# A third written order of all steps ahead of the experts, with the dilated unit 0 second

## The chip, the cores and the metric

The program runs on one core of a Trainium2 chip. The metric is the device time of one execution, in microseconds (us). The kernel before took 530.35 us, the median of three runs (530.16 to 531.51). One execution was profiled; its span is 528.5 us.

## What is computed

Attention over q, k, v of batch 2, 8 heads, 576 positions and depth 64: heads 0 to 3 see a plain causal window of 32, heads 4 to 7 a window of 128 in which every fourth position counts. Its 1152 x 512 result goes through a layer `h = x @ w_in` (512 x 1024), `solu = h * softmax(h)`, a layer norm over the 1024, scaled by g_ln, and `@ w_out` (1024 x 512). Four experts follow:

```
p = domain_probs / (domain_probs.sum(-1, keepdims=True) + 1e-09)
for e in range(4):
    h = np.maximum(x @ w1[e], 0.0)          # 512 x 1024
    out += p[:, e:e + 1] * (h @ w2[e])      # 1024 x 512
```

Every large product is done as three products of a high and a low part, so each weight and each activation is split in two before TensorE (PE) uses it.

## The kernel before

All that stands ahead of the experts is cut into steps, and one string, ORDER, lists them; a loop reads the string and lets each named generator run to its next `yield`. The order of the string is therefore the order in which instructions enter every engine's queue, and each engine works its own queue strictly in that order. SyncE (SP) issues every DMA. A "+" behind a step flips a switch for that one step: with it, some operations go to VectorE (DVE) in place of ScalarE (ACT), or to GpSimd (POOL) in place of DVE. The steps:

- `lP`, `lD`, `lvp`, `lvd` load q/k and v of one attention unit (L147, L150, L155). A unit is a third of the sequence of four heads of one batch: `UP.t.b` plain, `UD.t.b` dilated, 12 in all. In DMA names `qkD01` is batch 0, third 1.
- `UP`, `UD`: scores on PE (mask L262, q times k L271), maximum, subtraction, exponential, sum, reciprocal, division (L279, L281, L284, L286, L288, L290), the transpose of the weights on PE (L309, tile `pt`) or through memory, weights times v on PE (L320), and the split of the result into `xhi` (L170, L172) and `xlo` (L246). In this text QK, Tr and PV name the three PE parts.
- `lI.j`, `VI.j`: block j of w_in is loaded (L205, L208; 128 rows; block 0 in two halves, `lI.0` and `lI.4`) and converted from 64 bits: two ACT passes (L186, L188), two DVE operations (L190, L192), an addition (L194), then the split into `wh` (L172) and `wl` (L221). `lO`, `VO` do the same for w_out (`wh4` to `wh7`).
- `H.t`, t from 0 to 8: token tile t (128 rows) times w_in on PE (L350), four quarters, one for each block j; then maximum (L355), exponential (L357), product (L359), scaling (L362 on ACT or L364 on DVE).
- `T.t`: transpose of tile t. Tiles 3 to 8 go through memory: DVE shuffle into the one buffer `st4` (L395, L397), DMA out (L402, L405), ACT square (L407), DMA back into one of two `et` buffers (L411, L414), split into `hh` (L170, L172) and `hl` (L419).
- `X.c.d`: three token tiles times half of w_out on PE (L432), 48 matmuls in four parts of twelve, then the copy into `xf` (L170, L172).
- `F.n`: n matmuls on a constant tile (L84), whose result is not used.
- `WP`, `XQ`, `WV`, `u`, `d`: expert weights, split of xf, and the expert products on PE (L545, L617).

PSUM has two score/transpose buffers (`pa`) and two for H and X (`pm`); v of the plain units has two buffers (`vp`). A step that needs one waits for the reader of the one used two allocations before.

Of the kernel before, what the change touches and what calls it, by code (L numbers as in the profile page):

```python
# [27 lines left out]
ORDER = """
lP.0.0+ F.10 UP.0.0 UP.0.0+ lI.0 UP.0.0 lD.0.0 VI.0 VI.0 VI.0+ VI.0 F.4 UD.0.0 UP.0.0 UP.0.0+ lI.4 VI.0 VI.4+ UD.0.0 UP.0.0+ VI.4 UD.0.0+ UD.0.0+ lD.1.0+ VI.4
VI.4 VI.4+ lP.1.0+ F.3 UD.1.0 UD.1.0 UD.1.0+ UD.0.0 UD.0.0 UD.1.0+ UP.1.0 UP.1.0 UD.1.0 UD.1.0+ UP.0.0 VI.0 UP.1.0+ lD.2.0+ F.1 UD.2.0+ UD.2.0 lP.2.0 F.1  # L30
UP.2.0 UD.0.0+ UD.2.0 VI.4 UP.1.0+ UP.1.0+ lI.1+ UP.1.0+ VI.1+ VI.1+ UD.1.0+ lvd.1.0+ UP.2.0 UP.2.0+ UP.2.0 UD.1.0 VI.1+ VI.1 F.3 UP.0.0 UP.1.0 UD.1.0 VI.4+
F.1 UD.1.0+ UD.1.0+ UP.0.0 lI.2+ UD.1.0+ VI.0+ lvp.0.0+ UP.0.0 VI.2+ VI.2 UP.0.0 UP.0.0+ VI.1+ F.3 H.0+ VI.2 VI.2+ UD.2.0 VI.1 VI.1 UD.0.0 UD.0.0 UP.2.0+
UP.1.0 lI.3 UP.1.0 lvd.0.0 UD.0.0+ lvp.1.0 UP.1.0 lvp.2.0+ H.0+ UD.2.0+ VI.3 UD.0.0 UD.0.0 UP.1.0 UP.1.0 VI.3+ UD.2.0 VI.3 lP.0.1 UP.0.1 H.1 H.1 VI.2+ VI.2
UP.0.1 UP.0.1+ UP.0.1+ lO.0.0+ VO.0.0 VI.3 UD.2.0+ UD.2.0 UD.2.0 VI.3 VI.3 VI.3+ VI.2 lD.0.1+ UD.0.1 UD.0.1 UD.0.1+ lvp.0.1 lD.1.1+ UP.0.1 UP.2.0+ lvd.2.0+
UD.1.1 VO.0.0 lO.0.1 VO.0.1 UP.0.1 H.0 UD.1.1 VO.0.0 UD.2.0 UD.2.0 VO.0.0 VO.0.0+ H.0 UP.2.0+ lO.1.0+ lD.2.1 UD.2.0 H.0+ UD.0.1 UD.0.1+ endE+ UD.1.1+ VO.0.1+
VO.0.1+ H.0+ H.0 H.1 H.1 misc+ UP.0.1+ UP.0.1 UD.0.1+ UD.0.1+ H.1+ UP.2.0 UD.1.1 UD.0.1+ UD.0.1 UP.0.1 UP.0.1 UP.2.0 H.0+ UP.0.1 UP.0.1+ VO.0.1+ UD.1.1
lvd.1.1 UP.2.0 VO.0.1+ H.2 UP.2.0 lvd.0.1+ UP.2.0 UD.1.1 H.1+ H.1+ UD.1.1+ VO.0.0+ VO.0.0+ VO.0.1+ VO.0.1+ UD.2.1 UD.2.1+ VO.1.0+ VO.1.0 VO.1.0+ VO.1.0 lP.2.1
VO.1.0+ T.0 H.1+ lvp.2.1+ UD.2.1 lO.1.1+ UD.0.1+ T.0+ T.0 UD.1.1+ H.2+ H.2+ UD.2.1+ UD.1.1 T.1+ T.1+ T.1 H.3+ UD.2.1+ T.0+ UD.2.1+ T.1+ VO.1.0 VO.1.0+ VO.1.1+
VO.1.1 UP.2.1+ UP.2.1+ VO.1.1+ UP.2.1+ H.2+ UD.0.1 H.2 UD.0.1 lvp.1.1+ VO.1.1+ H.3+ UD.0.1+ lO.2.0+ VO.2.0 VO.2.0 UP.2.1 UP.2.1 UD.1.1 lP.1.1+ UD.2.1+ UD.2.1+
VO.1.1+ H.2+ H.3+ UD.1.1 UD.1.1 VO.2.0+ VO.2.0+ VO.2.0+ H.3 UD.1.1 H.3+ UP.2.1+ lO.2.1+ T.2 T.2 VO.1.1+ VO.1.1 T.2 T.2 VO.2.1+ VO.2.1+ UD.2.1+ VO.2.1+ H.4+  # L40
UP.2.1+ UP.2.1 H.4 H.4 UP.1.1+ VO.2.1+ UP.1.1+ UD.2.1+ UP.1.1 H.4 UP.1.1+ UP.1.1 UP.1.1 UP.1.1 X.0.1+ lO.3.0 VO.3.0 lvd.2.1 UP.2.1 VO.2.1+ UP.1.1+ VO.2.0+
VO.2.0 VO.2.1+ VO.2.1+ X.0.0 VO.3.0+ VO.3.0 VO.3.0+ VO.3.0 lO.3.1 VO.3.1 VO.3.1 UD.2.1+ VO.3.1+ VO.3.1 UP.2.1 VO.3.1 VO.3.0 H.4+ VO.3.1 VO.3.0+ VO.3.1 X.0.1+
UP.2.1 UP.1.1+ UP.1.1+ UD.2.1 UD.2.1 UP.1.1+ endA T.4 X.0.1 T.4+ T.4 H.3+ T.3+ T.3+ UP.1.1+ UP.1.1 H.5+ T.4+ T.3+ T.3+ H.5+ H.5+ H.5+ H.5+ H.5 X.0.0+ X.0.0
UP.2.1+ UP.2.1+ T.5+ T.5+ T.3+ H.6+ H.6+ T.4 T.4+ T.5 H.6 H.6+ T.3+ H.8 H.6 T.6 T.5+ T.6 H.8 H.8 T.5+ H.8+ H.8 T.8+ T.8+ T.6 T.6 H.7+ H.7 H.7 H.7 H.7 T.7+
T.7+ T.7+ T.6+ T.6 T.8+ T.8+ T.5+ X.1.0 X.1.0+ sc X.1.0 T.8+ T.8 T.7 X.1.1 X.1.1+ X.1.1 T.7+ T.7 endH XQ.0+ XQ.0 XQ.0 XQ.0 XQ.0 XQ.0 XQ.0 XQ.0 lW.0 WP.0+
WP.0+ WP.0 WP.0 WP.0 WP.0+ X.2.0 XQ.0 XQ.0 XQ.0 XQ.0+ XQ.0 XQ.0 XQ.0 WP.0+ WP.0 WP.0+ WP.0 WP.0 WP.0 WP.0+ WP.0 WP.0 X.2.1+ WP.0+ lW.1 WP.0 XQ.0 WP.0 X.2.0+
XQ.1 X.2.1 XQ.1 XQ.1 XQ.1 XQ.1 XQ.1 lV.0+ u.0+ u.0 u.0+ u.0 u.0 u.0+ u.0 u.0 u.0 endX u.0 u.0+ u.1+ u.0 XQ.1 XQ.1 u.1 WP.1+ WV.0 u.0+ u.0 u.0 WP.1 WV.0 u.0
u.0 u.0+ u.0 u.1+ u.0+ u.0+ u.0 u.0+ u.1 WV.0 WV.0 lV.1 u.0+ u.1+ u.1 lW.2 XQ.1 u.1+ u.1 XQ.1 XQ.1 XQ.1 d.2 d.2 XQ.1+ XQ.1 XQ.1 XQ.1+ WP.1+ d.0 d.0+ u.1+ u.1
u.1+ WP.1+ u.1+ u.1+ u.1+ u.1 u.1+ d.1+ d.1 WP.1 WP.1 u.1 u.1 u.1 u.1+ WP.1 WP.1+ WP.1 WP.1 WP.1 WP.1 WP.1+ WP.1 d.3+ WP.1 WP.1+ WP.1 d.3 WP.1 u.1 u.1 u.1+
u.1  # L50
"""
# [735 lines left out]
```

## Time and profile before

| what | value |
|---|---|
| median of three runs | 530.35 us |
| span of the profiled execution | 528.5 us |
| PE busy | 515.0 us (97%) |
| DVE busy | 356.9 us (68%) |
| ACT busy | 191.7 us |
| POOL busy | 187.3 us |
| DMA moved | 46.44 MB |

The page gives no total for the profiled execution besides its span; the median of the runs is 1.85 us above that span. PE busy counts the `F` matmuls too. Shares of the whole span hide the stages: PE is short of work ahead of about 30 us and has short gaps between 86 and 133 us, and from about 140 us, where the experts follow, it has none in the 20-us window shown below.

### The profile page before, as it was taken

What the parts mean: (1) busy time and instruction counts of PE and PEld (TensorE: products, weight loads), DVE (VectorE), ACT (ScalarE), POOL (GpSimd) and SP (SyncE); (2) the same over time, 40 slices, a digit from 0 to 9 for tenths busy, and PEclk for the clock granted to TensorE, in tenths of its full rate; (3) what the DMA queues carried; (4) which work ended last, traced back from release to release, by engine and by line L of the source; (5) the groups of instructions that cost most, each with busy time, mean ns of one, the idle gap of its engine ahead of it and who ended that gap; (6) DMA issues with size and microseconds to landing.
All of it is one profiled execution on the core that took longest, in us unless ns stands there. A gap on an engine that the chain in (4) does not pass through costs nothing.

```text
span 528.5 us, 9419 instructions
## 1 busy us (share of the span) xinstructions
PE 515.0 (97%) x3971; PEld 459.0 (87%) x3971; DVE 356.9 (68%) x474; ACT 191.7 (36%) x295; POOL 187.3 (35%) x130
## 2 busy tenths in 40 slices
...
GB/s 311 364 239 211 242 175 97 112 141 211 16 159 141 19 2 35 126 1 1 159 1 1 0 160 0 1 141 20 2 0 161 1 0 81 0 1 1 1 81 99
DMA packets 24490, 46.44 MB, mean 88 GB/s; under 512 B 4480, under 2 KB 9088, under 8 KB 24064
## 3 DMA queue, kind: packets, MB, share of 16 engines
...
## 4 chain that ended last, share of the span: by engine, by line
PE 87%; DMA 7%; DVE 4%; ACT 1%; SPq 1%; issue 0%; DVEq 0%; ACTq 0%
PE pa L617 19%; PE pm L617 18%; PE pm L545 17%; PE pa L545 17%; PE pm L350 7%; PE pm L432 6%; DMA vp<-in_vp_dram 2%; PE pa L320 2%; DMA et<-dt 2%; DMA draw<-in_moe_w_in_dram 1%; DMA dt<-st 1%; PE pa L271 1%; DVE e L359 1%; DVE e L364 1%; PE pa L381 1%; DVE st L397 0%
## 5 line engine op out<-in xcount | busy, mean ns | idle before, releaser
L558 DVE SCALAR_TENSOR_TENSOR hl<-ct,hh 128x512 fp32r<-128x512 f32 (+1 forms) x64 | 63.6, 1012 | 35.3 <-ACT hh L556 35.3
L556 ACT ACTIVATE hh<-ct 128x512 fp32r<-128x512 f32 (+1 forms) x64 | 42.1, 682 | 48.7 <-DVE ct L588 20.7
L617 PE MATMUL pa<-wl,hh 128*128 128x512 f32 (+1 forms) x148 | 57.3, 387 | 0.0
L617 PE MATMUL pa<-wh,hh 128*128 128x512 f32 (+1 forms) x148 | 57.3, 387 | 0.0
L617 PE MATMUL pa<-wh,hl 128*128 128x512 f32 (+1 forms) x148 | 57.1, 386 | 0.0
L545 PE MATMUL pm<-xoh,hl 128*128 128x256 f32 (+1 forms) x192 | 56.8, 296 | 0.0
L545 PE MATMUL pa<-xoh,hl 128*128 128x256 f32 (+1 forms) x192 | 56.8, 296 | 0.0
L545 PE MATMUL pm<-xol,hh 128*128 128x256 f32 (+1 forms) x192 | 56.8, 296 | 0.0
L545 PE MATMUL pa<-xol,hh 128*128 128x256 f32 (+1 forms) x192 | 56.8, 296 | 0.0
L545 PE MATMUL pm<-xoh,hh 128*128 128x256 f32 (+1 forms) x192 | 56.8, 296 | 0.0
L545 PE MATMUL pa<-xoh,hh 128*128 128x256 f32 (+1 forms) x192 | 56.8, 296 | 0.0
L617 PE MATMUL pm<-wl,hh 128*128 128x512 f32 (+1 forms) x144 | 55.7, 387 | 0.0
L617 PE MATMUL pm<-wh,hh 128*128 128x512 f32 (+1 forms) x144 | 55.7, 387 | 0.0
L617 PE MATMUL pm<-wh,hl 128*128 128x512 f32 (+1 forms) x144 | 55.6, 386 | 0.0
L464 POOL TENSOR_TENSOR wl<-wl,wh 128x1024 fp32r<-128x1024 f32 x7 | 16.9, 2414 | 95.3 <-ACT wh L172 95.3
L622 DVE SCALAR_TENSOR_TENSOR xf<-pm,pr,xf 128x512 f32<-128x512 f32 (+1 forms) x32 | 23.6, 738 | 31.1 <-PE pm L617 31.1
L464 POOL TENSOR_TENSOR hl<-sw,hh 128x512 fp32r<-128x512 f32 x22 | 33.5, 1522 | 30.3 <-ACT hh L172 27.6
L622 DVE SCALAR_TENSOR_TENSOR xf<-pa,pr,xf 128x512 f32<-128x512 f32 (+1 forms) x32 | 23.6, 738 | 30.3 <-PE pa L617 30.3
L172 ACT CAST wh<-wl 128x1024 fp32r<-128x1024 f32 x16 | 16.8, 1052 | 71.0 <-PE pa L617 40.5
L572 POOL TENSOR_TENSOR ct<-ct,ct 128x512 f32<-128x512 f32 (+1 forms) x15 | 21.4, 1426 | 48.1 <-ACT ct L570 42.9
L545 PEld LDWEIGHTS pm<-xoh,hh 128*128 128x128 f32 x192 | 36.4, 190 | 0.3
L545 PEld LDWEIGHTS pm<-xol,hh 128*128 128x128 f32 x192 | 36.4, 190 | 0.3
...
## 6 DMA issues: line engine op xcount, KB each, us to landing
...
```

What stands on the lines that cost most here:

```text
L172: nc.scalar.copy(out, in_)
L271: nc.tensor.matmul(ps[32 * g:32 * g + 32, j, 64 * m:64 * m + 64], lhsT=qt[rows, h, xq:xq + 32], rhs=kt[rows, h, xq:xq + 64], start=False, ...
L320: nc.tensor.matmul(po[64 * (g % 2):64 * (g % 2) + 64, j, o:o + 32], lhsT=vt[rows, m, g, :], rhs=pt[rows, m, g, :], start=True, stop=True)
L350: nc.tensor.matmul(pm[:, n, :], lhsT=xx[:, kk, cols], rhs=ww["in", kk][:, 512 * n:512 * n + 512], start=(n_ == 0 and i < 2), stop=(n_ == K ...
L432: nc.tensor.matmul(pm[:, dd, 0:CW], lhsT=w_, rhs=x_[:, f, :], start=(f == 0 and i == 0), stop=(f == KF - 1 and i == 2))
L464: pick().tensor_tensor(out=out, in0=a, in1=b, op=op)
L545: nc.tensor.matmul(ps[:, ff, 0:n], lhsT=a[:, kk, fc], rhs=b[:, kk, :], start=kk == 0 and m == 0, stop=kk == 1 and m == 2)
L556: nc.scalar.activation(out=hv, in_=src, func=AF.Relu)
L558: nc.vector.scalar_tensor_tensor(out=lv, in0=src, scalar=0.0, in1=hv.bitcast(F32), op0=ALU.max, op1=ALU.subtract)
L572: poolv().tensor_tensor(out=c12, in0=c21, in1=c22, op=ALU.add)
L617: nc.tensor.matmul(po[:, 0, 0:dn], lhsT=h_[:, f, cols], rhs=w_, start=(f == 0 and i == 0), stop=(f == 3 and i == 2))
L622: nc.vector.scalar_tensor_tensor(out=acc[:, t, dc], in0=po[:, 0, 0:dn], scalar=pr[:, t, e:e + 1], in1=acc[:, t, dc], op0=ALU.mult, op1=ALU ...
```

## The change

Only the string ORDER differs; every step of it is done in both kernels, 542 in each. The new string is one line shorter, so a line of the code has a number one less in the kernel after (L350 is L349). Its first line before and after:

```diff
-lP.0.0+ F.10 UP.0.0 UP.0.0+ lI.0 UP.0.0 lD.0.0 VI.0 VI.0 VI.0+ VI.0 F.4 UD.0.0 UP.0.0 UP.0.0+ lI.4 VI.0 VI.4+ UD.0.0 UP.0.0+ VI.4 UD.0.0+ UD.0.0+ lD.1.0+ VI.4
+lP.0.0+ lD.0.0 UP.0.0 lI.4 lD.1.0+ UP.0.0+ UD.0.0 F.3 lI.0 UP.0.0 UP.0.0 F.3 UD.0.0 VI.4+ lP.1.0+ lI.1+ UD.1.0 VI.4 VI.0 UP.0.0+ UP.0.0+ UD.0.0+ VI.4 VI.4
...
```

The F matmuls are 26 in both (10, 4, 3, 1, 1, 3, 1, 3 before; 3, 3, 1, 1, 1, 10, 4, 3 after). By the switches, DVE has 460 instructions where it had 465, POOL 134 for 127, ACT 274 for 276, in the part that the string orders.

First place: SP's queue of DMAs at the start of the program, before the change (`draw1` is block 1 of w_in, 1 MB; `draw0` has block 0 in two halves of 0.5 MB; a q/k unit is 0.43 or 0.46 MB, a v unit 0.39 MB):

```order
L147 DMA qkP00_107<-in_qkp_dram 128x832
L208 DMA draw0_202<-in_moe_w_in_dram 128x512
L147 DMA qkD00_110<-in_qkd_dram 128x896
L205 DMA draw0_202<-in_moe_w_in_dram 128x512
L147 DMA qkD01_111<-in_qkd_dram 128x896
L147 DMA qkP01_108<-in_qkp_dram 128x832
L147 DMA qkD02_112<-in_qkd_dram 128x896
L147 DMA qkP02_109<-in_qkp_dram 128x832
L208 DMA draw1_394<-in_moe_w_in_dram 128x1024
L150 DMA vd01_114<-in_vd_dram 128x768
L208 DMA draw2_455<-in_moe_w_in_dram 128x1024
L155 DMA vp_460<-in_vp_dram 128x768
L208 DMA draw3_520<-in_moe_w_in_dram 128x1024
L150 DMA vd00_113<-in_vd_dram 128x768
L155 DMA vp_550<-in_vp_dram 128x768
```

Here `qkD00` is third and block 1 of w_in ninth. SP's queue at the same place after the change:

```order
L146 DMA qkP00_107<-in_qkp_dram 128x832
L146 DMA qkD00_110<-in_qkd_dram 128x896
L204 DMA draw0_191<-in_moe_w_in_dram 128x512
L146 DMA qkD01_111<-in_qkd_dram 128x896
L207 DMA draw0_191<-in_moe_w_in_dram 128x512
L146 DMA qkP01_108<-in_qkp_dram 128x832
L207 DMA draw1_238<-in_moe_w_in_dram 128x1024
L146 DMA qkD02_112<-in_qkd_dram 128x896
L154 DMA vp_332<-in_vp_dram 128x768
L207 DMA draw2_410<-in_moe_w_in_dram 128x1024
L146 DMA qkP02_109<-in_qkp_dram 128x832
L149 DMA vd01_114<-in_vd_dram 128x768
L149 DMA vd00_113<-in_vd_dram 128x768
L154 DMA vp_458<-in_vp_dram 128x768
L154 DMA vp_482<-in_vp_dram 128x768
L146 DMA qkD10_119<-in_qkd_dram 128x896
L207 DMA draw3_558<-in_moe_w_in_dram 128x1024
```

Block 1 of w_in moves from ninth to seventh place, the dilated unit 0 from third to second, v of the plain unit 0 from twelfth to ninth, and q/k of the plain unit 2 (`qkP02`) from eighth to eleventh, behind three blocks of w_in; block 3 (`draw3`) moves from thirteenth to seventeenth.

Second place: PE around the first two quarters of H.0 (`wh0`, then `wh1`; `pa` rows are transposes, PVs and scores of attention units), before the change:

```order
L350 MATMUL pm_497<-wh0_206,xhi_90 128x512 x2
L350 MATMUL pm_497<-wl0_207,xhi_90 128x512 x2
L350 MATMUL pm_497<-wh0_206,xlo_91 128x512 x2
L309 MATMUL pa_509<-ident_74,pd1_126 128x128 x3
L309 MATMUL pa_516<-ident_74,pd0_125 128x128 x3
L320 MATMUL pa_525<-pt_513,vd00_113 64x32 x24
L320 MATMUL pa_552<-pt_522,vp_550 64x32 x24
L350 MATMUL pm_497<-wh1_397,xhi_90 128x512 x2
L350 MATMUL pm_497<-wl1_398,xhi_90 128x512 x2
L350 MATMUL pm_497<-wh1_397,xlo_91 128x512 x2
```

Between the two quarters stand two transposes and two PVs. PE around the same two quarters after the change:

```order
L270 MATMUL pa_431<-qkP02_109 32x64 x24
L308 MATMUL pa_465<-ident_74,pd2_127 128x128 x3
L349 MATMUL pm_473<-wh0_234,xhi_90 128x512 x2
L349 MATMUL pm_473<-wl0_235,xhi_90 128x512 x2
L349 MATMUL pm_473<-wh0_234,xlo_91 128x512 x2
L308 MATMUL pa_486<-ident_74,pd1_126 128x128 x3
L319 MATMUL pa_491<-pt_470,vd01_114 64x32 x24
L319 MATMUL pa_518<-pt_516,vd00_113 64x32 x24
L349 MATMUL pm_473<-wh1_335,xhi_90 128x512 x2
L349 MATMUL pm_473<-wl1_336,xhi_90 128x512 x2
L349 MATMUL pm_473<-wh1_335,xlo_91 128x512 x2
```

The second PV of a plain unit (`vp_550`) and one transpose no longer stand ahead of the second quarter; the scores of `qkP02`, which stood far ahead of the first quarter, now stand close before it.

Third place: PE where H.5 begins (`pm_1454`), before the change:

```order
L432 MATMUL pm_1232<-hh_942,wh7_1334 128x384
L432 MATMUL pm_1232<-hl_943,wh7_1334 128x384
L432 MATMUL pm_1232<-hh_942,wl7_1335 128x384
L320 MATMUL pa_1365<-pt_1330,vp_954 64x32 x24
L320 MATMUL pa_1397<-pt_1392,vp_1075 64x32 x24
L350 MATMUL pm_1454<-wh0_206,xhi_90 128x512 x2
L350 MATMUL pm_1454<-wl0_207,xhi_90 128x512 x2
L350 MATMUL pm_1454<-wh0_206,xlo_91 128x512 x2
L350 MATMUL pm_1454<-wh1_397,xhi_90 128x512 x2
```

X.0.1 (`pm_1232`) ends and two PVs follow before H.5. PE where H.5 begins (`pm_1301`) after the change:

```order
L431 MATMUL pm_1269<-hh_974,wh5_1081 128x384
L431 MATMUL pm_1269<-hl_975,wh5_1081 128x384
L431 MATMUL pm_1269<-hh_974,wl5_1082 128x384
L349 MATMUL pm_1301<-wh0_234,xhi_90 128x512 x2
L349 MATMUL pm_1301<-wl0_235,xhi_90 128x512 x2
L349 MATMUL pm_1301<-wh0_234,xlo_91 128x512 x2
L349 MATMUL pm_1301<-wh1_335,xhi_90 128x512 x2
L349 MATMUL pm_1301<-wl1_336,xhi_90 128x512 x2
L349 MATMUL pm_1301<-wh1_335,xlo_91 128x512 x2
```

H.5 stood behind both halves of X.0.1 and the last two PVs; it now stands between the two halves of X.0.1 (`pm_1269`), ahead of those PVs and of all of X.0.0. From H.6 on PE's order is the same in both: H.6, H.8, H.7, X.1.0, X.1.1, X.2.0, X.2.1, the expert products.

DVE's queue from the shuffle of tile 5 (`st4_1518`) to the maximum of H.7 (`pm_1607`), before the change:

```order
L395 STREAM_TRANSPOSE st4_1518<-e_1486 128x8x4x32
L170 CAST hh_1439<-et1_1471 128x8x128
L355 TENSOR_REDUCE nmx_83<-pm_1526 128x1
L359 SCALAR_TENSOR_TENSOR e_1551,nsum_85<-e_1551,pm_1526 128x1024
L364 TENSOR_SCALAR e_1551<-e_1551,nsum_85 128x1024
L397 STREAM_TRANSPOSE st4_1587<-e_1551 128x8x4x32
L355 TENSOR_REDUCE nmx_83<-pm_1559 128x1
L170 CAST hh_1439<-et1_1589 128x8x128
L359 SCALAR_TENSOR_TENSOR e_1593,nsum_85<-e_1593,pm_1559 128x1024
L364 TENSOR_SCALAR e_1593<-e_1593,nsum_85 128x1024
L397 STREAM_TRANSPOSE st4_1599<-e_1593 128x8x4x32
L355 TENSOR_REDUCE nmx_83<-pm_1607 128x1
```

Among the rows of tiles 6 and 8 stand two casts into `hh_1439`. DVE's queue from the shuffle of tile 5 (`st4_1487`) to the maximum of H.7 (`pm_1603`) after the change:

```order
L394 STREAM_TRANSPOSE st4_1487<-e_1450 128x8x4x32
L354 TENSOR_REDUCE nmx_83<-pm_1517 128x1
L358 SCALAR_TENSOR_TENSOR e_1543,nsum_85<-e_1543,pm_1517 128x1024
L363 TENSOR_SCALAR e_1543<-e_1543,nsum_85 128x1024
L396 STREAM_TRANSPOSE st4_1585<-e_1543 128x8x4x32
L354 TENSOR_REDUCE nmx_83<-pm_1557 128x1
L358 SCALAR_TENSOR_TENSOR e_1591,nsum_85<-e_1591,pm_1557 128x1024
L363 TENSOR_SCALAR e_1591<-e_1591,nsum_85 128x1024
L396 STREAM_TRANSPOSE st4_1600<-e_1591 128x8x4x32
L354 TENSOR_REDUCE nmx_83<-pm_1603 128x1
```

The two casts into `hh_1439` (tiles 3 and 5) are no longer in DVE's queue between these tiles; they are ACT's. The lo part of tile 6 (`hl`), which was DVE's behind H.7's work, is POOL's.

## Rows read from the trace of the kernel before

**Rows 1.** Windows of the span: PE, PEld, DVE, ACT, POOL busy; granted clock, DMA share, GB/s
```profile
10.00:20.00 10.00, 7.38 (x210) 4.48 (x210) 8.47 (x21) 5.50 (x10) 5.55 (x5) 0.83 1.03 414
...
20.00:30.00 10.00, 8.35 (x210) 6.80 (x211) 8.31 (x14) 7.88 (x13) 5.77 (x2) 0.83 0.82 299
...
60.00:80.00 20.00, 19.96 (x236) 17.49 (x235) 19.40 (x35) 14.46 (x25) 5.10 (x4) 1.00 0.55 174
...
140.00:160.00 20.00, 20.00 (x141) 20.00 (x141) 16.60 (x23) 9.55 (x14) 6.80 (x6) 1.00 0.31 106
```

**Rows 2.** PE's timeline up to 45 us: start, us, engine, line, operation, tiles
```profile
29.91 0.63 PE L350 MATMUL pm<-wl,xhi 128*128 128x512 f32 x2
...
30.90 0.33 PE L262 MATMUL pa<-mask,identb 128*128 128x192 bf16 x2
...
31.81 0.73 PE L350 MATMUL pm<-wh,xhi 128*128 128x512 f32 x2
...
39.84 0.62 PE L350 MATMUL pm<-wl,xhi 128*128 128x512 f32 x2
...
42.12 0.61 PE L350 MATMUL pm<-wh,xhi 128*128 128x512 f32 x2
...
43.49 0.82 PE L309 MATMUL pa<-ident,pd 128*128 128x128 f32 x6
...
44.55 1.60 PE L320 MATMUL pa<-pt,vp 64*64 64x32 f32 x96 [0.24 <-ACT pt L172]
```

**Rows 3.** ACT's timeline, the converting passes of w_in's blocks 1, 2 and 3
```profile
17.70 1.13 ACT L186 ACTIVATE draw<-draw 128x1024 int32<-128x1024 uint32 x1 [1.21 <-DMA draw<-in_moe_w_in_dram]
...
21.18 1.15 ACT L186 ACTIVATE draw<-draw 128x1024 int32<-128x1024 uint32 x1 [0.15 <-DMA draw<-in_moe_w_in_dram]
...
28.02 1.16 ACT L186 ACTIVATE draw<-draw 128x1024 int32<-128x1024 uint32 x1
```

**Rows 4.** SP's timeline, the longest wait of its queue ahead of 30 us
```profile
14.12 9.87 SPq L155 DMA_DIRECT2D vp<-in_vp_dram  x2
```

**Rows 5.** Groups by line and shape, 0 to 150 us: busy us, mean ns
```profile
L190 DVE TENSOR_SCALAR eva<-eva 128x1024 uint32<-128x1024 uint32 x2 | 1.4, 694 | 1.3 <-ACT eva L188 1.3
...
L192 DVE SCALAR_TENSOR_TENSOR eva<-draw,eva 128x1024 uint32<-128x1024 uint32 x2 | 2.4, 1222 | 0.0
...
L246 DVE TENSOR_TENSOR xlo<-pa,xhi 128x384 fp32r<-128x384 f32 x10 | 6.7, 678 | 1.8 <-ACT xhi L172 1.6
...
L281 DVE TENSOR_TENSOR sm<-pa,st 128x384 f32<-128x384 f32 x12 | 6.7, 558 | 0.3
...
L288 DVE RECIPROCAL st<-st 128x6 f32<-128x6 f32 x12 | 2.2, 186 | 0.1
```

**Rows 6.** PE's timeline, 86 to 133 us, rows after a wait and two ahead of one
```profile
86.67 0.73 PE L350 MATMUL pm<-wh,xhi 128*128 128x512 f32 x2 [0.92 <-ACT xf L172]
...
112.80 0.41 PE L432 MATMUL pm<-hh,wh 128*128 128x384 f32 x1
...
114.02 0.44 PE L432 MATMUL pm<-hl,wh 128*128 128x384 f32 x1 [0.82 <-POOL hl L419]
...
130.43 0.34 PE L432 MATMUL pm<-hh,wl 128*128 128x384 f32 x1
...
131.75 0.41 PE L432 MATMUL pm<-hh,wh 128*128 128x384 f32 x1 [0.98 <-ACT xf L172]
...
132.96 0.44 PE L432 MATMUL pm<-hl,wh 128*128 128x384 f32 x1 [0.80 <-DVE hl L419]
```

**Rows 7.** DVE's timeline, 112 to 120 us
```profile
112.69 1.84 DVE L364 TENSOR_SCALAR e<-e,nsum 128x1024 f32<-128x1024 f32 x1
...
115.73 1.19 DVE L355 TENSOR_REDUCE nmx<-pm 128x1 f32<-128x1024 f32 x1
...
119.51 0.75 DVE L364 TENSOR_SCALAR e<-e,nsum 128x1024 f32<-128x1024 f32 x1
```

**Rows 8.** POOL's timeline, the lo part of tile 5
```profile
111.59 2.38 POOL L419 TENSOR_TENSOR hl<-et,hh 128x1024 fp32r<-128x1024 f32 x1 [7.31 <-DVE hh L170]
```

More of the change, by code (lines that the diff above doesn't have):

```diff
@@ L28 @@
 ORDER = """
-lP.0.0+ F.10 UP.0.0 UP.0.0+ lI.0 UP.0.0 lD.0.0 VI.0 VI.0 VI.0+ VI.0 F.4 UD.0.0 UP.0.0 UP.0.0+ lI.4 VI.0 VI.4+ UD.0.0 UP.0.0+ VI.4 UD.0.0+ UD.0.0+ lD.1.0+ VI.4
-VI.4 VI.4+ lP.1.0+ F.3 UD.1.0 UD.1.0 UD.1.0+ UD.0.0 UD.0.0 UD.1.0+ UP.1.0 UP.1.0 UD.1.0 UD.1.0+ UP.0.0 VI.0 UP.1.0+ lD.2.0+ F.1 UD.2.0+ UD.2.0 lP.2.0 F.1
-UP.2.0 UD.0.0+ UD.2.0 VI.4 UP.1.0+ UP.1.0+ lI.1+ UP.1.0+ VI.1+ VI.1+ UD.1.0+ lvd.1.0+ UP.2.0 UP.2.0+ UP.2.0 UD.1.0 VI.1+ VI.1 F.3 UP.0.0 UP.1.0 UD.1.0 VI.4+
-F.1 UD.1.0+ UD.1.0+ UP.0.0 lI.2+ UD.1.0+ VI.0+ lvp.0.0+ UP.0.0 VI.2+ VI.2 UP.0.0 UP.0.0+ VI.1+ F.3 H.0+ VI.2 VI.2+ UD.2.0 VI.1 VI.1 UD.0.0 UD.0.0 UP.2.0+
@@ L33 @@
[L33 to L48, printed above, removed]
@@ L49 @@
-u.1+ WP.1+ u.1+ u.1+ u.1+ u.1 u.1+ d.1+ d.1 WP.1 WP.1 u.1 u.1 u.1 u.1+ WP.1 WP.1+ WP.1 WP.1 WP.1 WP.1 WP.1+ WP.1 d.3+ WP.1 WP.1+ WP.1 d.3 WP.1 u.1 u.1 u.1+
-u.1
+lP.0.0+ lD.0.0 UP.0.0 lI.4 lD.1.0+ UP.0.0+ UD.0.0 F.3 lI.0 UP.0.0 UP.0.0 F.3 UD.0.0 VI.4+ lP.1.0+ lI.1+ UD.1.0 VI.4 VI.0 UP.0.0+ UP.0.0+ UD.0.0+ VI.4 VI.4
+UP.0.0+ UD.1.0 UD.1.0+ VI.0 VI.0+ VI.4+ UP.1.0 VI.0 UD.0.0+ UD.1.0+ lD.2.0+ VI.4 UP.1.0 UP.1.0+ VI.0+ UD.0.0 UP.0.0 F.1 UP.0.0 UP.1.0+ VI.4+ F.1 UD.1.0 UD.1.0+
+VI.0 F.1 lvp.0.0+ VI.0 VI.1+ F.10 UP.1.0+ VI.1+ UD.0.0 UD.1.0+ UD.2.0+ VI.1+ UD.0.0+ UP.1.0+ UP.0.0 VI.1 UP.1.0+ lI.2+ VI.1+ lP.2.0 VI.2+ UD.2.0 UP.0.0+
```

18 lines of the change are left out of this document (added).

## The prediction

> **What bounds the kernel now.** I read the windows of the span first. From 140 us on PE is busy 20.00 of 20.00 us [rows 1], so the expert part is held by PE's own work; ahead of it PE has holes: 7.38 of 10 us busy at 10 to 20 and 8.35 of 10 at 20 to 30 [rows 1], part of that being F matmuls that nobody uses, and then single waits at 86.67, 114.02, 131.75 and 132.96 [rows 6]. The useful matmuls are the same in both orders. The end therefore moves by as much as PE's waits ahead of the first expert product change, and I work them out in three stages. A time below is on the clock of the profiled span; a difference found on it is put on the median of 530.35 us, which is 1.85 above the span of 528.5.
>
> What sets the first stage is read from PE's timeline together with ACT's and DVE's rows: the second quarter of H.0 reaches its `wl` matmuls at 29.91 [rows 2], and these need block 1 of w_in, whose ACT passes start at 17.70, when its DMA lands [rows 3]. In the last stage the reader is to see that PE waits there for the chain behind one token tile: the `hl` of tile 5 (114.02), the copy of X.1.1 into xf (131.75) and the `hl` of the last tile (132.96) [rows 6].
>
> **Early stage: block 1 sooner, blocks 2 and 3 and one unit later.** By the sizes of the DMAs, block 1 was complete after 4.75 MB of SP's queue and is now after 3.87. Between 10 and 20 us the queue moves 414 GB/s [rows 1]; 0.88 MB less is 2.1 us, so it lands at 15.6 in place of 17.70. Two ACT passes of about 1.14 [rows 3] end at 17.9. From there DVE works down its new queue to `wl1`: two shifts of 0.69, two merges at 1.22, one addition and the `wl` subtraction of the same size costed alike, one xlo at 0.68, six operations on one unit's scores at 0.56 and two reciprocals at 0.19 [rows 5]: 1.4 + 4.9 + 0.7 + 3.4 + 0.4 = 10.7, so `wl1` is there at 28.6, 1.3 ahead of the 29.91 of before. But PE has done less by then: one transpose and one PV, which stood ahead of this quarter, come later now. Half of 0.82 and half of 1.60 [rows 2] is 1.2. Net about -0.1; with the transposes spaced more closely than their busy time it may be -0.3. I take **-0.2**.
>
> Two things in this chain have little room. The chain reaches the first reduction for `qkP02` at about 22.9, and `qkP02`, now behind 6.19 MB, lands at 21.2 (before, block 2 ended after just that many bytes and its pass began at 21.18 [rows 3]); its scores take 0.9 (30.90 to 31.81 [rows 2]), which leaves 0.7. Block 3, thirteenth in the queue before, is now seventeenth: 3.08 MB behind that point, 7.4 us at 414 GB/s, so 28.6. Before, its passes began at 28.02 [rows 3] and its `wl` was used at 39.84 without a wait [rows 2], 11.8 later; the same way puts `wl3` at 40.4 at the latest. PE from `wl1` on has the rest of the quarter (1.0), four scores of 0.91, three transposes of 0.41, two PVs of 0.80, three quarters of 1.37 (42.12 to 43.49) and the start of the fourth (0.5) [rows 2]: 12.1, so it asks at 40.7. Covered, by 0.3. If the queue moves at the 299 GB/s of 20 to 30 us [rows 1], block 3 lands at 31.5, and PE waits 2.6. That slow window holds a stall, though: SP stood 9.87 us in front of a v buffer [rows 4]; now v of the plain unit 0 is loaded and used first, and the third v is asked for after it is free. So I go by 414. The bounds of this stage are -1.3 (the whole advance of `wl1` stays) and +2.6.
>
> The F matmuls keep their number but sit elsewhere. The granted clock is 0.83 in both 10-us windows from 10 to 30 us and 1.00 later [rows 1], between the levels of 1.2 and 2.4 GHz; so each window holds some 3.4 us at the lower one. What is slow there is mostly work with a wait behind it; I cost it at nothing, with 0.5 either way.
>
> **Middle stage.** DVE loses five instructions, POOL gains seven. PE is busy 19.96 of 20.00 us from 60 to 80 [rows 1], so what DVE sheds (some 3 us, at the 0.56 of [rows 5] or more for each) has nothing to give there. The one wait is the 0.92 in front of H.5 for the copy of X.0.1 into xf [rows 6]: that copy is released only when the two PVs behind X.0.1 are done, and H.5 takes the buffer that it frees. Now X.0.0 takes that buffer, behind the same two PVs. The wait moves, it doesn't go: **0**, bounds -0.9 and +1.0 (the same wait a second time, since H.5 now holds the other buffer while X.0.1 is unfinished).
>
> **Late stage.** From H.6 on PE's order is the same; only what lies ahead differs. H.5 is what tile 5 waits for. Between its end and X.1.0 stood half of X.0.0 and three tiles of H; the 94 matmuls of X.1.0 and X.1.1 from 114.02 to 130.43 [rows 6] give 0.175 for each, so 24 of them are 4.2, and a tile is four quarters of 1.37: 4.2 + 16.4 = 20.6 us. The chain of tile 5 runs from H.5's start at 86.67 [rows 6] to the end of its `hl` on POOL (111.59 + 2.38 [rows 8]), 27.3 us, of which H.5 itself is 5.5: 21.8 after its end. The difference is the wait at 114.02: 1.22 from the matmul at 112.80 in place of 0.175, so 1.05 lost [rows 6]. Now the other half of X.0.1, two PVs and all of X.0.0 follow H.5 as well: 4.2 + 1.6 + 8.3 + 16.4 = 30.5 us for the same chain. Even with DVE working tiles in another order this is covered: **-1.05**.
>
> The other two waits are tile 7's. H.7 ends where X.1.0 begins, at 112.80 [rows 6]; its maximum starts at 115.73 [rows 7], 2.9 late, as DVE still had the shuffle of tile 8 in front of it, behind a scaling that took 1.84 where the same form took 0.75 [rows 7]. From H.7's end to the `hl` used at 132.96 it is 20.1 us. The PE work that hides it is X.1.0 and X.1.1, 16.7. Of the two casts that went from DVE to ACT here one stood between tiles 6 and 8, and tile 6's `hl` left DVE; without the slow scaling another 1.1 goes. I let the maximum start 0.3 to 1.3 after H.7's end, which makes the chain 17.5 to 18.5 and the wait 0.8 to 1.8 where all three together cost 1.05 + 1.15 (130.43 to 131.75) + 1.04 (131.75 to 132.96) = 3.24 [rows 6]. With 1.2 left the stage gains **-2.0**; its bounds are -3.2 (no wait is left) and 0 (tile 7's chain grows by what tile 5's wait gives back).
>
> The slow scaling at 112.69 lies under POOL's `hl` of 111.59 to 113.97 [rows 7, 8], and it ends late by just the stretch in which both run. The Trainium skill, "SBUF — State Buffer", section "Who interferes with whom", has a rule for this: VectorE and GpSimd share a pair of ports, and whoever holds it keeps the other out for its whole instruction. The trace agrees at this place (1.84 for 0.75). It speaks against the change, since POOL gets seven more instructions, one of them tile 6's `hl`. By it that `hl` of 2.4 us would hold up a DVE instruction of tile 8 or 7 by about 1.1 again, and tile 7's wait would be 1.8 rather than 1.2.
>
> **Sum.** -0.2 + 0 - 2.0 = -2.2 on 530.35, which gives 528.1 us. I allow the early stage its -0.3 and predict 528.0.
>
> **Rivals.**
> First, slower: the DMA queue. Three blocks of w_in now stand ahead of `qkP02`, whose scores stand ahead of all of H on PE, and block 3 is four places later. If `qkP02` lands after about 23, or block 3 after 31, PE waits 2.6 at H.0's fourth quarter or before its first, and what DVE and ACT have behind it is late too. With half of the late gain this is 530.35 + 3.2 - 1.0, about 532.5. For it: the margins are 0.7 and 0.3, and the rows of 20 to 30 us have 299 GB/s. Against it: the stall of 9.87 that this window held is not in the new queue.
> Second, no change: early -0.2, and late nothing, since tile 8's and tile 7's last four DMAs are issued behind each other at the end of SP's queue and POOL has tile 6: X.1.0 is met, X.2.0 waits 3 us instead of 2. About 530.1. For it: PE reaches X.2.0 sooner by 1.05 when the wait ahead of X.1.0 goes, so tile 7's chain must be shorter by that much only to stay level. Against it: the 2.9 late start has named causes which leave DVE.
> Third, more: `wl1`'s advance stays whole (-1.3) and no late wait is left (-3.2): 525.9. For it: DVE has less work, and if nothing else binds early, the two pieces of PE work left for later fill holes. Against it: 17.5 is still over 16.7.
>
> **How the numbers follow.** The forecast has 0.43, the slower rival 0.17, no change 0.20, more 0.20. A measurement of this kernel can tell about 0.3%, 1.6 us, from no change: faster is below 528.8, slower above 531.9. The forecast's own spread (527.2 to 529.0) falls under faster for all but 0.04, the slower rival reaches down into no change by little: 0.59 faster, 0.25 same, 0.16 slower. The range goes from 525.6, just past the third, to 532.2, most of the way into the first.
>
> **What would show it.** In the profile of the changed kernel: the converting pass of block 1 starting at about 15.6 on ACT; the `wl` matmul of H.0's second quarter at 28 to 29; no wait above 0.5 at H.0's fourth quarter; no wait for tile 5's `hl` at the start of X.1.0; one wait of 0.8 to 1.8 at X.2.0; the 0.9 for xf in front of X.0.0. It is wrong if `qkP02`'s scores start after 23 us, if H.1 ends later than 43.5 on PE, if X.2.0 still waits over 2 us, or if PE has a wait among the first expert products that it had not before.

## The result

The kernel after took 536.93 us (median of four runs, 536.41 to 538.64), the kernel before 530.25 beside it: a ratio of 1.014, 95% interval 1.0106 to 1.0173. The change made the kernel 6.7 us slower; 528.0 was forecast, with a range up to 532.2. Its profiled execution spans 534.6 us, 6.1 more than the one of before.

Three places in PE's order with the same matmuls ahead of them tell where the time went. The start of H.6 moved from 96.43 to 99.92 us (+3.5), the start of X.1.0 from 112.80 to 116.28 (+3.5), the first expert product from 149.54 to 155.41 (+5.9). So 3.5 us were lost ahead of H.6 and 2.4 between X.1.0 and the experts, and almost nothing after them. Within the first part, H.1 ends at 48.83 for 43.49; PE has done one score and one transpose more by then (1.3 us), which leaves a loss of 4.0, of which the stretch up to H.6 gave back 0.5. PE's rows at the start of H.6 and of the first expert product, before and after:

```profile
96.43 0.62 PE L350 MATMUL pm<-wh,xhi 128*128 128x512 f32 x2
...
149.54 0.28 PE L545 MATMUL pa<-xoh,hh 128*128 128x256 f32 x1
```

```profile
99.92 0.63 PE L349 MATMUL pm<-wh,xhi 128*128 128x512 f32 x2
...
155.41 0.28 PE L544 MATMUL pa<-xoh,hh 128*128 128x256 f32 x1
```

One window of the kernel before, then four of the kernel after, with the columns of [rows 1]:

```profile
40.00:60.00 20.00, 19.76 (x323) 16.17 (x323) 19.49 (x35) 17.92 (x31) 7.96 (x8) 1.00 0.71 241
```

```profile
20.00:30.00 10.00, 6.81 (x163) 5.56 (x164) 9.36 (x17) 8.61 (x13) 5.17 (x3) 0.91 1.00 394
...
40.00:60.00 20.00, 17.42 (x311) 14.18 (x310) 16.61 (x33) 14.10 (x24) 7.39 (x6) 1.00 0.79 260
...
120.00:140.00 20.00, 16.45 (x87) 15.94 (x87) 14.67 (x20) 6.18 (x10) 7.27 (x4) 0.94 0.51 145
140.00:160.00 20.00, 20.00 (x127) 20.00 (x126) 15.17 (x19) 5.89 (x9) 10.16 (x7) 0.98 0.24 82
```

PE is idle 3.2 us from 20 to 30 (1.7 before [rows 1]), 2.6 from 40 to 60 and 3.6 from 120 to 140. The middle one is new: in the same window of before PE was busy 19.76 of 20.

**Block 3 of w_in came when the prediction said, block 1 sooner.** ACT's rows that answer to [rows 3], blocks 1, 2 and 3:

```profile
15.71 1.18 ACT L185 ACTIVATE draw<-draw 128x1024 int32<-128x1024 uint32 x1
...
20.32 1.15 ACT L185 ACTIVATE draw<-draw 128x1024 int32<-128x1024 uint32 x1 [2.40 <-DMA draw<-in_moe_w_in_dram]
...
28.91 1.18 ACT L185 ACTIVATE draw<-draw 128x1024 int32<-128x1024 uint32 x1
```

Forecast were 15.6 for block 1 and 28.6 for block 3. Only the row of block 2 shows a wait for its DMA. Block 3's landed at 28.89 by its semaphore in the trace, and its pass began at once. Block 1's landed at 14.71; ACT was at other work until 15.71, so that the pass began at the forecast time is chance. The scores of `qkP02` started at 21.75 without waiting for their data (PE had waited 2.00 us until 21.48 for DVE to free the scores' buffer).

DVE's `wl1`, before and then after:

```profile
26.52 1.22 DVE L221 TENSOR_TENSOR wl<-eva,wh 128x1024 fp32r<-128x1024 f32 x1
```

```profile
26.61 1.22 DVE L220 TENSOR_TENSOR wl<-eva,wh 128x1024 fp32r<-128x1024 f32 x1
```

It was ready at 27.83 (forecast 28.6), and before at 27.74, 2.2 ahead of the 29.91 at which PE used it. PE was busy with its own queue then, so the prediction's "1.3 ahead of the 29.91 of before" compares a time of PE with a time of DVE: `wl1` did not come sooner than before.

**But PE stopped twice around it.** PE's timeline of the kernel after: the two dilated PVs (48 matmuls each), H.0's second quarter, the scores and PV of two later dilated units, and the row behind the end of H.1:

```profile
24.60 1.48 PE L319 MATMUL pa<-pt,vd 64*64 64x32 f32 x87
27.78 0.36 PE L319 MATMUL pa<-pt,vd 64*64 64x32 f32 x9 [1.70 <-issue]
28.07 1.11 PE L349 MATMUL pm<-wh,xhi 128*128 128x512 f32 x2
28.98 1.05 PE L349 MATMUL pm<-wl,xhi 128*128 128x512 f32 x2
...
41.71 0.73 PE L270 MATMUL pa<-qkD 64*32 64x64 f32 x48 [1.23 <-DMA qkD<-in_qkd_dram]
43.78 0.90 PE L319 MATMUL pa<-pt,vd 64*64 64x32 f32 x48 [1.34 <-DMA vd<-in_vd_dram]
...
48.83 0.49 PE L308 MATMUL pa<-ident,pd 128*128 128x128 f32 x3
```

The reader is to see three things. The second PV breaks off after 87 of the pair's 96 matmuls for 1.70 us, "issue": the profile shows no engine and no DMA that released it. The quarter behind it takes 1.05 to 1.11 a row where such rows took 0.61 to 0.73 before [rows 2]; the granted clock is 0.55 from 28 to 30 us, mostly the level of 1.2 GHz; the quarter ends at 30.69. And at 41.71 and 43.78 PE waits for q/k of `UD.2.1` and for v of `UD.2.0`. SP's queue says why these are late:

```profile
12.17 6.08 SPq L154 DMA_DIRECT2D vp<-in_vp_dram  x2
...
22.34 0.33 SPq L146 DMA_DIRECT2D qkD<-in_qkd_dram  x1
35.10 0.33 SPq L154 DMA_DIRECT2D vp<-in_vp_dram  x1
35.47 1.43 SPq L146 DMA_DIRECT2D qkD<-in_qkd_dram  x1
36.95 0.91 SPq L149 DMA_DIRECT2D vd<-in_vd_dram  x2
```

Between 22.7 and 35.1 us SP issues nothing: it stands in front of `vp`, v of the plain unit 0 of batch 1, whose buffer is free only when the PV at 34.13 has run (plain unit 1 of batch 0). The two late loads were behind it, and the DMA queues ran dry meanwhile (105 GB/s from 30 to 40 us). The stall of [rows 4], which the prediction took as gone, is in the first row: 6.08 us in place of 9.87, with the queues still at 410 GB/s from 10 to 20 us.

**In the last stage one wait went and another grew.** PE's rows that answer to [rows 6]:

```profile
91.49 0.44 PE L431 MATMUL pm<-hh,wh 128*128 128x384 f32 x1 [0.92 <-ACT xf L171]
...
116.28 0.33 PE L431 MATMUL pm<-hh,wh 128*128 128x384 f32 x1
116.59 0.44 PE L431 MATMUL pm<-hl,wh 128*128 128x384 f32 x1
...
135.15 0.41 PE L431 MATMUL pm<-hh,wh 128*128 128x384 f32 x1 [1.81 <-ACT xoh L171]
137.29 0.53 PE L431 MATMUL pm<-hl,wh 128*128 128x384 f32 x1 [1.74 <-DVE hl L418]
137.62 0.52 PE L431 MATMUL pm<-hh,wl 128*128 128x384 f32 x1
```

At X.1.0 the second matmul follows after 0.31; the wait for tile 5's `hl` is gone but for 0.14. At X.2.0 PE now waits 1.81 for tile 7's `hh` and 1.74 for its `hl` (the first row names ACT's `xoh`, which X.2.0 does not read; of what it reads tile 7's `hh`, on DVE up to 134.94, came last). Behind that the matmuls start 0.32 apart in place of 0.175, and PE is at the level of 1.2 GHz up to 140.8 (granted clock 0.57 from 137 to 141). DVE and POOL in the same stretch, for [rows 7, 8]:

```profile
118.29 1.19 DVE L354 TENSOR_REDUCE nmx<-pm 128x1 f32<-128x1024 f32 x1
...
122.08 2.67 DVE L363 TENSOR_SCALAR e<-e,nsum 128x1024 f32<-128x1024 f32 x1
...
131.86 1.22 DVE L169 CAST hh<-et 128x1024 fp32r<-128x1024 f32 x1 [0.76 <-DMA et<-dt]
...
134.25 0.69 DVE L169 CAST hh<-et 128x1024 fp32r<-128x1024 f32 x1
134.97 2.18 DVE L418 TENSOR_TENSOR hl<-et,hh 128x1024 fp32r<-128x1024 f32 x1
```

```profile
121.79 2.40 POOL L418 TENSOR_TENSOR hl<-et,hh 128x1024 fp32r<-128x1024 f32 x1 [5.25 <-ACT hh L171]
...
131.24 1.28 POOL L463 TENSOR_TENSOR ct<-xf 128x512 f32<-128x512 f32 x1 [1.45 <-DVE xf L169]
134.31 1.75 POOL L463 TENSOR_TENSOR ct<-xf,ct 128x512 f32<-128x512 f32 x1 [1.79 <-ACT xf L171]
```

Each slow row of DVE lies under a row of POOL: the scaling of tile 7 takes 2.67 (0.75 alone, [rows 7]) under tile 6's `hl`, tile 8's cast 1.22 (0.69 for the next one) under a `ct`, tile 7's `hl` 2.18 (1.23 for tile 8's, in the trace) under the next `ct`.

### The profile page after: what moved, and what is told of

Same layout as the page of the kernel before. It is cut to its first block, busy times and chain, and to the rows that moved or that the text cites. A ratio compares the mean times of both kernels' runs of the same rounds, so it can differ in the third digit from the quotient of the medians.

```text
span 534.6 us, 9428 instructions
## 1 busy us (share of the span) xinstructions
PE 514.4 (96%) x3971; PEld 459.7 (86%) x3971; DVE 354.4 (66%) x469; ACT 189.4 (35%) x293; POOL 198.0 (37%) x137
## 4 chain that ended last, share of the span: by engine, by line
PE 76%; DVE 8%; DMA 7%; ACT 4%; issue 2%; SPq 1%; POOL 0%; DVEq 0%; ACTq 0%
PE pa L616 19%; PE pm L616 18%; PE pm L544 17%; PE pa L544 17%; PE pm L431 3%; DMA dt<-st 2%; DMA draw<-in_moe_w_in_dram 2%; DMA et<-dt 1%; DMA vd<-in_vd_dram 1%; ACT e L356 1%; PE pm L349 1%; DVE st L396 1%; DVE e L358 1%; DVE e L363 1%; DVE nmx L354 1%
## 5 line engine op out<-in xcount | busy, mean ns | idle before, releaser
L557 DVE SCALAR_TENSOR_TENSOR hl<-ct,hh 128x512 fp32r<-128x512 f32 (+1 forms) x64 | 61.7, 982 | 33.1 <-ACT hh L555 33.1
L463 POOL TENSOR_TENSOR hl<-sw,hh 128x512 fp32r<-128x512 f32 x21 | 30.9, 1469 | 33.3 <-ACT hh L171 24.0
L571 POOL TENSOR_TENSOR ct<-ct,ct 128x512 f32<-128x512 f32 (+1 forms) x16 | 23.7, 1480 | 47.7 <-ACT ct L569 47.7
```

Source lines behind the costliest of these rows:

```text
L463: pick().tensor_tensor(out=out, in0=a, in1=b, op=op)
L557: nc.vector.scalar_tensor_tensor(out=lv, in0=src, scalar=0.0, in1=hv.bitcast(F32), op0=ALU.max, op1=ALU.subtract)
L571: poolv().tensor_tensor(out=c12, in0=c21, in1=c22, op=ALU.add)
```

## The experiments

The theory after the comparison has three separate causes. SP's wait for a v buffer holds up two loads (some 2.7 us). PE runs out of instructions in a PV, and its clock falls behind the idle time. POOL's work beside DVE lengthens tile 7's chain, and again the clock falls behind the wait. Ratios are to the kernel before on the same chip; the kernel after, unchanged, was run again among them:

> The kernel after, unchanged, beside the others on one chip. Expected: 1.2 to 1.6% above the kernel before, and again a stop of PE in the middle of the second dilated PV after 87 of 96 matmuls if the instruction packet is late in this execution too (the theory allows its length to differ, since it depends on how full the DMA queues are; a rival that lays it to one disturbed execution has it gone).

It took 1.0145 of before (1.0095 to 1.0196), with a stop of 2.03 us after 87 of the pair's 96 matmuls again. Its wait for v was 2.5 us there.

**SP's wait.** One load moved:

```diff
-... H.1 UP.2.0 lvp.0.1 UP.0.1 lD.2.1 lvd.2.1 ... lvd.2.0+ UP.0.1+ ...
+... H.1 UP.2.0 UP.0.1 lD.2.1 lvd.2.1 ... lvd.2.0+ lvp.0.1 UP.0.1+ ...
```

> The kernel after, with one load moved in SP's queue: v of the plain unit 0 of batch 1 (lvp.0.1) is asked for behind the other loads (q/k of the dilated units 1 and 2, v of the dilated units) that stood behind it. Theory: SP stood from 22.8 to 35.1 us in front of that load's buffer, and qkD of unit 2 (landed 41.7) and v of the dilated unit 2 (landed 43.6) were late for that alone. Then both land before 36, PE's waits of 1.23 and 1.34 at 41.71 and 43.78 go, H.1 ends about 2.7 earlier (46.1 for 48.8), and the whole is 2 to 2.7 faster than the kernel after: 534.3 to 535. Rival: the loads are late since the DMA queues are full; then they land after 40 again and the time is that of the kernel after within 0.5.

Measured: 1.0061 (1.0042 to 1.008), so 0.8% or 4.2 us faster than the kernel after; its execution spans 528.3. SP's queue in it:

```profile
22.96 1.35 SPq L149 DMA_DIRECT2D vd<-in_vd_dram  x2
33.42 0.33 SPq L154 DMA_DIRECT2D vp<-in_vp_dram  x1
```

The wait for the buffer is still there (9.1 us, from 24.3 to 33.4), but the loads of q/k and v stand ahead of it, PE's waits at 41.71 and 43.78 are gone and H.1 ends at 44.60 in place of 48.83. The two v loads landed at 33.7 and 34.7, so the rival (full DMA queues) is out. The gain was 2.0 to 2.7 by the theory, and why it is larger is only in part seen. In other executions with the load in its old place the wait for v was longer than in the profile above (2.2 and 2.5 us) with slow rows behind it. The profiled execution is no fair measure: it is the fastest of twelve (530.09 us, median 533.30), it had no long stop in the PV, and it took 36.9 us from X.1.0 to the first expert product where the kernel after took 39.1, though nothing is changed there.

**The stop in the PV.** Two kernels that change only the number of unused F matmuls, `F.10` to `F.20` in the one, `F.10`, `F.4` and `F.3` left out in the other.

> The kernel after, with ten more unused F matmuls (20 for 10) ahead of the scores of the dilated unit 2: 20 more PE instructions ahead of the place where PE stopped for 1.70 us in the middle of a PV (after 87 of 96 matmuls, at 26.08). Theory: PE had no further instructions, since the 16 KB instruction packet that began at 25.40 was late. The place is then set by the count of PE instructions: it moves back by 20 of them, ten matmuls earlier, so the PVs stop after 77 of 96 matmuls. Rival: PE was held there by another engine's work (DVE's wl of block 1 ended at 27.8) or by v's landing; then it stops after 87 again, or not in the PV at all.

PE's timeline of the kernel with 20:

```profile
23.73 1.35 PE L319 MATMUL pa<-pt,vd 64*64 64x32 f32 x77
27.64 0.54 PE L319 MATMUL pa<-pt,vd 64*64 64x32 f32 x19 [2.56 <-issue]
```

It breaks off after 77 of 96: twenty PE instructions more ahead of it (each matmul comes with a weight load), ten matmuls sooner in the PV, as the theory says and no rival does. One execution, so no verdict on the time: 535.58 us.

> The kernel after without the three F steps ahead of H.0 (17 matmuls, 34 PE instructions fewer). Theory of the late instruction packet: the place lies 34 instructions later in the program, which is inside H.0's second quarter or behind it, where PE goes slowly; no stop in the PV, the quarter's wh matmuls start at about 26.1 in place of 28.07, the wl ones at 27.8 in place of 28.98, and the clock does not fall behind it: 1.2 to 3.4 us earlier at H.1's first quarter, if the missing F don't lower the clock before. Whole: 1 to 3 faster than the kernel after. Rival (held by another engine): the quarter starts at 28 again, same time.

Measured: 1.0076 (1.0057 to 1.0094), 3.4 us faster than the kernel after, and no stop in the PVs. But the gain didn't come on the way that was expected:

```profile
23.92 1.06 PE L349 MATMUL pm<-wl,xhi 128*128 128x512 f32 x2
...
26.40 1.80 PE L319 MATMUL pa<-pt,vd 64*64 64x32 f32 x96
28.13 0.72 PE L349 MATMUL pm<-wh,xhi 128*128 128x512 f32 x2
```

In this execution PE is at 1.2 GHz up to about 27 us (granted clock 0.50 from 14 to 26 and 0.78 from 26 to 28; 1.06 a row in H.0's first quarter), and the quarter starts at 28.13, no sooner. What is better is that it and what follows run at 2.4 GHz. The clock had fallen ahead of the first of the missing F, so that they are the cause is not shown.

To see what the stop itself costs, the second PV was put behind the quarter, in the kernel after and in a version with the edits on the late stage (below):

```diff
-... UD.0.0 UD.0.0+ UD.1.0 VI.1 UD.1.0+ H.0+ VI.2 ...
+... UD.0.0 UD.1.0 VI.1 UD.1.0+ H.0+ UD.0.0+ VI.2 ...
```

> The kernel after with one step moved: the PV of the dilated unit 0 stands behind H.0's second quarter, no longer directly behind the other dilated PV. Theory of the late instruction packet: PE's instructions run out at the same count, now some 33 matmuls into that PV, but PE gets there only behind the quarter, which waits for block 1's wl until 27.8 anyway; so no stop of 1.7 to 2.5 us inside a PV, the quarter's wh matmuls start ahead of 26.5 and the clock, if the idle time is what lowers it, stays up in the 3 us behind. Alone it gains 0.5 to 2.5 us on the kernel after (1.4% above before becomes 1.0 to 1.3%), unless the wait for v of the dilated unit 2 at 43.7 swallows it: then the same within 0.3%. Rival: the stop has another cause and stands behind the quarter or in front of the PV again.

> The best version so far (v asked for later, tile 6's hl and the two ct on DVE) with that PV behind the quarter too. With the wait for v gone the gain can reach H.1: its end at 44.0 to 45.2 for 45.68, the whole 0.2 to 0.5 % below that version, 525.5 to 528. If DVE's queue is what sets H.0's later quarters (the xlo of the moved PV comes later and holds up what is behind it), nothing or a loss of up to 1.

Measured: 1.0103 (1.0049 to 1.0157) for the first, not to be told from the kernel after; 0.9985 (0.9952 to 1.0017) for the second, no better than without that edit. No stop in the PV in either, but PE stands idle all the same (PE's timeline of the second):

```profile
27.35 0.73 PE L349 MATMUL pm<-wh,xhi 128*128 128x512 f32 x2
29.64 1.22 PE L349 MATMUL pm<-wl,xhi 128*128 128x512 f32 x2 [1.56 <-DVE wl L220]
30.66 1.05 PE L349 MATMUL pm<-wh,xlo 128*128 128x512 f32 x2
```

The quarter's first rows go early, and then PE waits 1.56 for `wl1`, which DVE finishes no sooner; the clock falls as before, and stays down to 40 us. In the kernel after, too, `wl1` was ready only at 27.83, and the stop ended at 27.78. So the stop for instructions was mostly time that PE would have waited for DVE. What is left to blame is the fall of the clock behind the idle time, whatever it is that PE waits for, and the last run of this line fills that time:

```diff
-... UD.1.0+ H.0+ UD.0.0+ VI.2 ...
+... UD.1.0+ F.6 H.0+ UD.0.0+ VI.2 ...
```

> The version with the PVs apart and the three other edits, and six unused F matmuls (1.3 us) in front of H.0's second quarter, where PE stood idle 1.6 to 1.7 us for block 1's wl. Theory: that idle time is what lowers PE's clock behind it (in both profiled runs with the PVs apart 1.2 GHz from the wl matmuls on for about 9 us). Filled, the idle time there falls to under 0.6, the quarter's wl and xlo rows go at 2.4 GHz (0.62 a row for 1.05), H.0's third quarter starts 3 to 4 us earlier, and the whole is 0.4 to 0.8% below the version without (0.9985 of before), so 0.990 to 0.995. Rival: the clock falls for what lies further back (the waits ahead of 22 us); then the rows behind are slow again and the time is the same within 0.3%.

PE's timeline:

```profile
27.48 0.82 PE L349 MATMUL pm<-wh,xhi 128*128 128x512 f32 x2
28.81 0.73 PE L349 MATMUL pm<-wl,xhi 128*128 128x512 f32 x2 [0.51 <-DVE wl L220]
29.37 0.62 PE L349 MATMUL pm<-wh,xlo 128*128 128x512 f32 x2
...
32.77 0.52 PE L308 MATMUL pa<-ident,pd 128*128 128x128 f32 x3 [1.02 <-DVE xlo L245]
```

The idle time is 0.51, the rows behind are at 0.62, and the granted clock is 1.00 from 22 to 40 us. From the quarter's `wl` rows to the end of H.1 it is 18.7 us (28.81 to 47.49) for 21.8 (29.64 to 51.39). That much is as the theory says, in one profiled execution each. The time is 0.9963 (0.9947 to 0.9979), 0.2% below the version without the F, where 0.4 to 0.8 were expected, and the two intervals overlap, so a gain is not shown. The profile without the F is of an execution of 535.40 us, the slowest of twelve whose median is 529.12: the 3.1 us are not what the clock costs in most executions, and how much it does stays open. A wait of 1.02 for the moved PV's xlo at 32.77 takes a part.

**Tile 6's `hl`.** One switch:

```diff
-... T.7+ T.7+ T.6+ T.8+ ...
+... T.7+ T.7+ T.6 T.8+ ...
```

> The kernel after, with one switch turned: the lo part of tile 6 (hl) is DVE's again and stands behind tile 7's shuffle there. Theory: POOL's hl at 121.79 to 124.2 made DVE's scaling of tile 7 take 2.67 for 0.75; without it the scaling takes 0.75, tile 7 leaves for memory 1.9 earlier, and X.2.0 starts 1.9 earlier; the wait for hl at 137.29 (1.74) stays, as POOL's ct still lies under tile 7's hl. Whole: 1.5 to 2.5 faster than the kernel after. Rival: the four last DMA reads in SP's queue set tile 7's landing; then it stays at 131.8 and the time is the same within 0.5.

Measured: 1.0041 (1.002 to 1.0062), 1.0% or 5.2 us faster than the kernel after, more than twice what was expected. DVE's and PE's timelines:

```profile
125.30 0.75 DVE L363 TENSOR_SCALAR e<-e,nsum 128x1024 f32<-128x1024 f32 x1
...
136.59 1.22 DVE L418 TENSOR_TENSOR hl<-et,hh 128x1024 fp32r<-128x1024 f32 x1
```

```profile
136.77 0.41 PE L431 MATMUL pm<-hh,wh 128*128 128x384 f32 x1 [0.22 <-PE pm L431]
137.87 0.44 PE L431 MATMUL pm<-hl,wh 128*128 128x384 f32 x1 [0.69 <-DVE hl L418]
```

The scaling takes 0.75 and tile 7's `hl` 1.22; PE's two waits are 0.22 and 0.69 for 1.81 and 1.74 (the second was expected to stay), and the clock does not fall behind them. From X.1.0's start to the first expert product it is 34.8 us for 39.1. The 1.9 of the scaling, 1.0 of the `hl` (POOL's `ct` now starts at 137.53, near its end) and 1.6 of clock are about that. The rival (the last DMA reads) is out.

**Together.** The two edits, then with the two `ct` on DVE as well (`XQ.0+ XQ.0+` to `XQ.0 XQ.0`), and that one a second time:

> The kernel after with both edits: v of the plain unit 0 of batch 1 asked for later, and tile 6's hl on DVE. If the two losses are separate (one ahead of 45 us, one behind 115) their gains add: 0.8% and 1.0% off the kernel after, so 0.4% below to level with the kernel before (527.5 to 530). If what is won early is given back late (DVE or the DMA reads set X.2.0 by themselves) it is no faster than the one edit on tile 6, 531.

> As the run before, and the two subtractions for the experts (ct) that POOL did beside tiles 8 and 7's casts are DVE's, behind tile 7's hl. Theory of the shared path of DVE and POOL: tile 8's cast into hh takes 0.69 for 1.25, tile 7's hl 1.22 at any place of the ct, so X.2.0's waits get shorter by 0.5 to 1.5 and PE's loss behind 130 us is under 1; whole 0.1 to 0.3% below the run before. Rival: tile 8's landing sets it and the cast just starts a wait; then the same within 0.1%, or slower as DVE has 1.4 us more ahead of the first expert product.

> The version that was below the kernel before (v later, tile 6's hl and the ct on DVE), again and beside the one above: 0.992 to 0.998 of the kernel before.

Measured: 0.9971 (0.9946 to 0.9996), 0.995 (0.9921 to 0.9978) and 0.9976 (0.9954 to 0.9997). The gains add (1.0140 less 0.8% and 1.0% is 0.996), and the result is 0.2 to 0.5% below the kernel before: 528.8, 528.6 and 528.2 us. The forecast of 528.0 was 0.9956 of it. From the 1.0140 of the kernel after to 0.9971 the two edits take away 1.7 of the 1.8% by which it was missed. The `ct` edit alone can't be told from nothing in the times; in the profile tile 8's cast takes 0.69 again for 1.04, and from X.1.0 to the first product it is 34.9 us for 35.5.

## Why the prediction was wrong, step by step

- Right: where block 3 lands (28.9 for 28.6), that `qkP02` is no bound, that tile 5's wait goes (1.05 forecast, 0.9 measured, as 0.14 is left), that the wait for xf only moves (0.92 at 91.49). The middle stage, forecast at 0, gave back 0.5. `wl1` was ready at 27.83 for 28.6, but no sooner than before (27.74), so the 1.3 of advance in the early sum was never there.
- The step that failed first is the early sum's "it asks at 40.7", which has no wait of PE between `wl1` and H.0's last quarter. PE came there at 45.18. The sum followed SP's queue up to block 3 and no further, and took the 9.87 us stall of [rows 4] as gone. Four rows later in the same queue another v load waits 12.4 us for a PV, with two loads behind it that PE needs ahead of H.0's last quarter. It is the very PV (`vp_550` before) that the sum booked as work that "comes later now": it freed the buffer by 29.4 before, and by 35.1 after. The forecast counted the moved loads themselves, not what queues behind the one that waits. Price: 2.7 in the profile, 4.2 in the times.
- The clock was costed at nothing with 0.5 either way. It cost 1.5 at 28 to 32 us and 1.6 at 137 to 141: both times it fell where PE had just been idle 1.7 us or more, and in the one profiled execution with the first idle time filled it did not fall there. That such a wait lowers it is not shown as a rule. In the kernel after PE was idle 2.00 us ahead of 21.48 and the granted clock stayed at 1.00 up to 28 us, and in the profile with the v load moved waits of 1.19 and 1.88 at X.2.0 had no slow rows behind them. Waits in this kernel can cost more than they last.
- The step that failed late is the sum's chain of tile 7. It let the maximum of H.7 start 0.3 to 1.3 after H.7's end and the chain take 17.5 to 18.5. The maximum started 2.0 after (118.29; before 2.9), and the chain took 20.9, from 116.28 to 137.15. The rows under POOL account for it: 1.92 + 0.53 + 0.95 = 3.4, and without them 17.5. The prediction saw such a price and sized it at 1.1, but left it out of its sum. The 1.1 came from one overlap in which POOL was half done when the scaling began, and it was not the length of the overlap, as the prediction has it (112.69 to 113.97 is 1.28). The scaling ended 0.56 us behind POOL's row in both kernels (114.53 behind 113.97, 124.75 behind 124.19). So the price hangs on where the two begin, and here it was 1.9. What was left out was to look which of POOL's seven new instructions would stand beside DVE's in that chain. By the Trainium skill, "SBUF — State Buffer", section "Who interferes with whom", the engine that issues first has the shared pair of ports for its whole instruction and blocks the other. The trace agrees in kind: the scaling that began 0.29 us behind POOL's row ended only behind that row.
- The wait at 131.75 of [rows 6] was read as one for the copy of X.1.1 into xf, as the row names it. X.2.0 takes the buffer of X.1.0, whose copy into xf began at 123.67; what came just ahead of 131.75 is tile 7's `hh`, on DVE from 130.95 to 131.64. So that wait, too, belongs to tile 7's chain.
- The slower rival had the right stage and the wrong place: block 3 and `qkP02`, for which PE did not wait. The margin of 0.3 for block 3 did not hold, though: its `wl` was forecast at 40.4 at the latest and came from POOL at 41.88 (row below), later than the 40.7 at which PE was to ask; PE, held up elsewhere, used it at 45.18. The rival also kept half of the late gain, and none was there.

```profile
39.47 2.41 POOL L220 TENSOR_TENSOR wl<-eva,wh 128x1024 fp32r<-128x1024 f32 x1 [1.16 <-ACT wh L171]
```

Two of the prediction's own signs of being wrong came true: H.1 ended at 48.83 (43.5 was the limit), and X.2.0 waited 3.55 us (limit 2).
